# Order within the steps of a one-core attention and MLP kernel: magnitudes behind the activation, k'v copied out a step later, normalisation a step behind its statistics, row loads together, jobs at other steps

## The chip, the cores and the metric

One Trainium2 chip; the program runs on one core. The metric is the device time of that core in microseconds. Three runs of the kernel before gave 1775.66 to 1778.61 us, median 1776.37 us.

## The reference

All tensors are float32. Three stages follow each other (cut to what is computed):

```python
# q, k, v: (8 batches, 8 heads, 576 rows, 64); g_norm: (64,)
kv  = einsum('bhsd,bhse->bhde', k, v)
out = einsum('bhsd,bhde->bhse', q, kv)
x   = out / sqrt(mean(out*out, -1) + 1e-6) * g_norm      # heads side by side: (8, 576, 512)

u   = x + real(fft(fft(x, axis=1), axis=2))
un  = (u - mean(u)) / sqrt(var(u) + 1e-6)                # over the 512 columns
x   = u + relu(un @ moe_w_ch1) @ moe_w_ch2               # 512 -> 2048 -> 512

u   = x + (x^T @ U @ V)^T                                # over the 576 rows, rank 32
out = u + relu(u @ moe2_w_ch1) @ moe2_w_ch2              # 512 -> 2048 -> 512
```

The weights of the first MLP are drawn eight times larger than those of the second.

## The kernel before

The 8 x 576 = 4608 rows are cut into nine blocks of 512 (`NB = 9`). The first MLP takes one block in 16 steps (`NF = 16`), one step for 128 of the 2048 hidden columns. The steps are counted through: block j, step i is n = 16 j + i.

In step n TensorE first multiplies the normalised block by 128 columns of the first weight (`emit_l1(n)`, 12 matmuls of 128x512 into `h`), and then adds the product of the step before to the output (`emit_l2(n - 1)`, into four `acc` banks that live for the whole block). A product of two float32 matrices is made of three products of split operands (L224 to L226 and L253 to L255): a high part that ScalarE rounds off (`w1h`, `w2h`, `gh`, `xh`) and a remainder (`w1l` on POOL, in some steps on DVE; `w2l`, `gl`, `xl` on DVE). For the steps in the list `PLAIN`, the second product is not split: ScalarE makes one `g` (L229), TensorE multiplies four float32 pairs (L245), and no `w2h`, `w2l`, `gl` is made.

Every other stage is cut into small tasks that stand in the list `side[n]` and are emitted at the end of step n, behind `emit_l2(n - 1)`; `fill[n]` stands ahead of `emit_l2(n - 1)`. While block j is in the MLP, the tasks of batch j + 1 run: q times k'v (`o`, L358), its norm (squares L360, sums L365, power on POOL L367, scaling L376 and L378), the Fourier transform by folds (`f`, `e`, `eh`, `ez`) and two table products (`t_s1`, L437 to L443; `t_s2`, L469 to L471) whose parts are added up (`y`, `de`, `x`) and stored to HBM as `u_d`. At the end of a block the next block's rows are loaded back (`t_ln_load`: `un<-u_d`), their mean and variance taken (`t_ln_stats`, L577 and L578), normalised (`t_ln`: power on POOL L583, `un` L585) and transposed (`t_tr`: `tr` L595, then `xh` and `xl`). `t_kv` multiplies k' by v for a later batch (10 matmuls for each half, L298) and copies the diagonal blocks out to `kvbd` (ScalarE L302, DVE L306). The side products share two PSUM banks.

The first weights come as 64-bit words and are converted in the kernel: `w_mags` takes the magnitude of the low word on ScalarE (L113, L114), `convert` puts the parts together on DVE (L122 to L130) and POOL (L130), and `w_next` starts the load of a later piece. `w_conv` does this for the first MLP in the side tasks of block 0; `w_pre` does it for the second MLP's weights in steps `PRE` of the blocks 1 to 6 and stores the result (`wb_d`). From block 7 on the rank-32 stage and the second MLP run beside the rest; a `job` combines outputs that are needed for it in three side tasks of successive steps (DVE L878, L883, L893).

The order on each engine is the order in which the program emits: no scheduler reorders it, and each engine takes its instructions in turn. So a task that stands earlier in a list holds up everything behind it on its engines. TensorE, ScalarE (ACT), VectorE (DVE), GpSimd (POOL) and the DMA queue on SyncE (SP) run beside each other and wait by semaphores.

The last blocks of the program are one more block of 16 steps for the second MLP and four `group` passes for the rest of its rows.

Of the kernel before, what the change touches and what calls it, by code (L numbers as in the profile page):

```python
# [34 lines left out]
EARLY = (2, 3, 4)  # L35
PLAIN = (0, 1, 2, 3, 4, 5, 6, 7, 8, 12, 13)

# [8 lines left out]
def kernel(ctx: ExitStack, tc: tile.TileContext, qT, kvm, gn, w1a, w2a, w1b, w2b,  # L46
# [111 lines left out]
    def w_conv(*ss):  # L158

        convert(*((raws.pop(s), w_new(s), pws.pop(s)) for s in ss))  # L160
        w_next(ss)
        w_mags(*(s + 2 for s in ss if s + 2 < 2 * NF))

    pws = {}

    def w_mags(*ss):
        for s in ss:
            pws[s] = conv_0(raws[s], s % 4 > 1)
# [121 lines left out]
    kvbd = com.tile([128, 4, 128], F32, tag="kvbd", name="kvbd")  # L290

    def t_kv(b, half):
        kv = st[b]["kv"]
        ps = side_bank(f"kv{b}_{half}")
        for j in range(2):
            cols = slice(256 * half + 128 * j, 256 * half + 128 * j + 128)
            for t in range(KC):
                nc.tensor.matmul(out=ps[:, 128 * j:128 * j + 128], lhsT=kv[:, 0, t, cols], rhs=kv[:, 1, t, cols],  # L298
                                 start=(t == 0), stop=(t == KC - 1))
        pv = ps[:, 0:256].rearrange("p (j e) -> p j e", j=2)  # L300
        pairs = slice(2 * half, 2 * half + 2)
# [201 lines left out]
    def batch_tasks(b):  # L503
# [14 lines left out]
        for p in range(2):  # L518
            t[8 if d else 7 + p] += [lambda p=p, e=e: t_s1(b, p, e) for e in range(2)]
        if b + 1 < B:  # L520
            if b + 1 in EARLY:
                t[11].insert(0, lambda: kv_back(b + 1))
            else:
                t[7].append(lambda: load_kv(b + 1))
                t[11].insert(0, lambda: t_kv(b + 1, 0))
                t[12].insert(0, lambda: t_kv(b + 1, 1))
            t[12].append(lambda: load_q(b + 1))
# [25 lines left out]
    def t_ln_load(j):  # L553
        un_new(j)
        for t in range(4):
            load_u(un[j][t], 4 * j + t)
# [554 lines left out]
    side = {n: [] for n in range(-NF, NA + NF)}  # L1111
    CONV = 13
    on_dve = set()
    ONDVE = (3, 4)
    PRE = (0, 9, 12)
    SH = 1
# [5 lines left out]
    with tc.manual_schedule():  # L1122
# [16 lines left out]
        def conv(k):  # L1139
            nonlocal done  # L1140
            for _ in range(k):
                w_conv(done, done + 1)
                done += 2

        t_kv(0, 0)
# [50 lines left out]
        side[3].append(lambda: kv_load_early(4, 11))  # L1196
        fill = {n: lambda b=b, h=h: t_kv_early(b, h) for n, b, h in ((7, 4, 0), (8, 4, 1))}

        for j in range(NB):
            n0 = j * NF  # L1200
            if j + 1 < NB:
                side[n0 + 12].append(lambda j=j: t_ln_load(j + 1))
                side[n0 + 13].append(lambda j=j: (t_ln_stats(j + 1, range(4)), t_ln(j + 1)))
            if j + 1 < B:
                place(batch_tasks(j + 1), n0)
                on_dve |= {n0 + k for k in ONDVE if j}
            side[n0 + 13].append(lambda j=j: [t_res(j, t) for t in range(4)])
        side[7 * NF].append(lambda: t_mu(0))
# [4 lines left out]
        for e in range(4):  # L1213
            side[NA + 11 + e].append(lambda e=e: t_xsum(NB, e))
        place(prep_b(0), NA - NF)
        starts = [7 * NF + k for k in (5, 7, 9, 14)] + [8 * NF + k for k in (1, 3, 5, 7, 9, 11, 13, 15)] + \
                 [NA + k for k in (1, 3, 5, 7)]
        for k, n in enumerate(starts):
# [22 lines left out]
        for c in range(4):  # L1241
            side[NA + 12 + c].append(lambda c=c: v_load(c))
        for k, m in enumerate(range(done, 2 * NF, 2)):
            side[k * CONV * 2 // (2 * NF - done)].append(lambda m=m: w_conv(m, m + 1))
        spots = [NF * j + i for j in range(1, 8) for i in PRE]
# [11 lines left out]
        for n in range(NP):  # L1257
            i, j = n % NF, n // NF
            split_w2(n)
            emit_l1(n)  # L1260
            if n + 2 < NP:
                split_w1(n + 2)
# [134 lines left out]
```

## Time and profile before

| | |
|---|---|
| median of three runs | 1776.37 us |
| the profiled execution | 1777.05 us, of it the traced span 1775.1 us |
| TensorE busy in the span | 1717.9 us (97%) |
| DVE, ACT, POOL busy | 1187.7, 824.4, 464.6 us |
| mean granted TensorE clock | 0.987 of full speed |
| chain of waits, share of the span | TensorE 78%, DVE 12%, DMA 3%, ACT 3% |

TensorE is busy nearly all the time, so a microsecond is to be had where it stands idle, where its clock is granted at the lower level, or where it is given less work. Its idle time adds up to 57 us, 39 us of that in the first 205 us. Times in the rows are in microseconds from the start of the span. A row of a stretch of instructions gives the start, the duration, the engine, the line, the operation with the tiles it writes and reads, how many like instructions in a row it stands for, and in brackets how long the engine was idle before and what ended that.

### The profile page before, as it was taken

To read this page: it belongs to the slowest core of one execution; us is meant where nothing else is said; L and a number is where in the kernel's file an instruction comes from. 1 tells how busy PE (TensorE), PEld (TensorE's weight loads), DVE (VectorE), ACT (ScalarE), POOL (GpSimd) and SP (SyncE) were. 2 spreads that over 40 slices of the span, in tenths; PEclk is the share of its full clock that TensorE was granted. 3 is DMA by queue.
4 is the path that set the end of the run, shared out by engine and by line. 5 is a ranking of instruction groups with operands and counts; after the bars stand their busy time and mean duration, and the time that the engine had idled before them with its cause. 6 is when DMAs were issued, how large, how long until landed. Compare 5 with 4: busy or idle time off the path is not lost.

```text
span 1775.1 us, 22909 instructions
## 1 busy us (share of the span) xinstructions
PE 1717.9 (97%) x8092; PEld 1421.3 (80%) x8092; DVE 1187.7 (67%) x1906; ACT 824.4 (46%) x1579; POOL 464.6 (26%) x368
## 2 busy tenths in 40 slices
PE   5888999999999999999999999999999999999999
PEld 5657688888888888888888878888888888888887
DVE  5777777868667585774476676637934873595286
ACT  3565444544444344443445465355535644453343
POOL 2454445554444554444222222100000000000000
PEclk7999999999999999999999999999999999999999
DMA  9654305133242413402258885567785776677676
GB/s 372 242 178 148 139 24 186 51 117 119 107 151 96 165 69 119 150 1 87 78 184 301 289 306 196 184 204 224 232 280 176 250 254 207 212 239 240 197 224 192
DMA packets 129683, 318.97 MB, mean 180 GB/s; under 512 B 20680, under 2 KB 23512, under 8 KB 127328
## 3 DMA queue, kind: packets, MB, share of 16 engines
q1 hardware_dynamic: 129568, 317.51, 53.5%
q8 instruction: 64, 1.05, 0.2%
q14 instruction: 51, 0.42, 0.1%
HBM read 241.52 MB, written 77.57 MB: 180 GB/s over the span
## 4 chain that ended last, share of the span: by engine, by line
PE 78%; DVE 12%; DMA 3%; ACT 3%; issue 2%; POOL 2%; SPq 0%; ACTq 0%; DVEq 0%; POOLq 0%
PE y L1020 10%; PE yy L1100 10%; PE h L224 6%; PE h L225 6%; PE h L226 5%; PE acc L253 5%; PE acc L255 5%; PE acc L254 5%; PE z L1100 5%; PE zz L1020 5%; PE w L1100 2%; PE z L1020 2%; DVE f L397 2%; PE o L358 2%; DVE f L392 1%
## 5 line engine op out<-in xcount | busy, mean ns | idle before, releaser
L200 POOL TENSOR_TENSOR w1l<-w,w1h 128x512 fp32r<-128x512 f32 x148 | 200.1, 1352 | 434.3 <-ACT w1h L199 417.5
L224 PE MATMUL h<-xl,w1h 128*128 128x512 f32 x576 | 230.6, 400 | 1.4 <-DVE xl L600 1.4
L226 PE MATMUL h<-xh,w1l 128*128 128x512 f32 x576 | 225.0, 391 | 0.5 <-POOL w1l L200 0.5
L225 PE MATMUL h<-xh,w1h 128*128 128x512 f32 x576 | 225.3, 391 | 0.0
L253 PE MATMUL acc<-w2h,gl 128*128 128x512 f32 x532 | 210.1, 395 | 8.7 <-DVE gl L234 8.6
L255 PE MATMUL acc<-w2h,gh 128*128 128x512 f32 x532 | 207.7, 390 | 0.0
L254 PE MATMUL acc<-w2l,gh 128*128 128x512 f32 x532 | 207.7, 390 | 0.0
L1020 PE MATMUL y<-xv,v 128*128 128x512 f32 x768 | 187.4, 390 | 2.7 <-ACT g L957 2.7
L233 ACT ACTIVATE gh<-h 128x512 fp32r<-128x512 f32 x149 | 88.5, 594 | 193.3 <-PE h L226 180.2
L957 ACT ACTIVATE g<-y 128x512 f32<-128x512 f32 x128 | 76.6, 598 | 204.0 <-PE y L1020 204.0
L1020 PEld LDWEIGHTS y<-xv,v 128*128 128x128 f32 x768 | 143.8, 188 | 34.1 <-ACT g L957 4.4
L234 DVE SCALAR_TENSOR_TENSOR gl<-h,gh 128x512 fp32r<-128x512 f32 x149 | 102.1, 685 | 87.8 <-ACT gh L233 86.6
L210 DVE TENSOR_TENSOR w2l<-w,w2h 128x512 fp32r<-128x512 f32 x149 | 132.0, 886 | 23.5 <-ACT w2h L209 22.6
L226 PEld LDWEIGHTS h<-xh,w1l 128*128 128x128 f32 x576 | 108.5, 188 | 24.3 <-POOL w1l L200 0.9
L224 PEld LDWEIGHTS h<-xl,w1h 128*128 128x128 f32 x576 | 108.7, 189 | 23.7 <-DVE xl L600 1.8
L253 PEld LDWEIGHTS acc<-w2h,gl 128*128 128x128 f32 x532 | 100.3, 188 | 33.4 <-DVE gl L234 13.2
L225 PEld LDWEIGHTS h<-xh,w1h 128*128 128x128 f32 x576 | 108.8, 189 | 21.7 <-issue 1.4
L255 PEld LDWEIGHTS acc<-w2h,gh 128*128 128x128 f32 x532 | 100.2, 188 | 21.1
L254 PEld LDWEIGHTS acc<-w2l,gh 128*128 128x128 f32 x532 | 100.3, 189 | 20.1
L199 ACT ACTIVATE w1h<-w 128x512 fp32r<-128x512 f32 x160 | 99.7, 623 | 24.0 <-DVE w L130 24.0
L209 ACT ACTIVATE w2h<-w 128x512 fp32r<-128x512 f32 x149 | 92.9, 623 | 37.0 <-PE acc L255 33.5
L951 DVE TENSOR_TENSOR g<-zz,g 128x512 f32<-128x512 f32 x64 | 44.2, 691 | 89.8 <-ACT g L957 77.4
(219 smaller groups left out, 3642.1 us busy)
## 6 DMA issues: line engine op xcount, KB each, us to landing
v<-wv_d SPq DMA_DIRECT2D x224, 512.0 KB, 4.1
wv_d<-vo SPq DMA_DIRECT2D x112, 256.0 KB, 2.7
kv<-in_kvm SPq DMA_DIRECT2D x8, 1280.0 KB, 8.1
q<-in_qT SPq DMA_DIRECT2D x8, 1220.0 KB, 9.6
x_d<-x2o SPq DMA_DIRECT2D x36, 256.0 KB, 2.0
x2f<-x_d SPq DMA_DIRECT2D x36, 256.0 KB, 5.5
outT<-o SPq DMA_DIRECT2D x36, 256.0 KB, 2.7
u_d<-x SPq DMA_DIRECT2D x32, 256.0 KB, 2.8
```

Source lines behind the costliest of these rows:

```text
L199: nc.scalar.activation(out=ah, in_=a, func=AF.Copy)
L200: (nc.vector if n in on_dve else nc.gpsimd).tensor_tensor(out=al, in0=a, in1=f32(ah), op=ALU.subtract)
L210: nc.vector.tensor_tensor(out=cl, in0=c, in1=f32(ch), op=ALU.subtract)
L224: nc.tensor.matmul(out=h, lhsT=ah[:, kc, :], rhs=xl[:, kc, :], start=(kc == 0), stop=False)
L225: nc.tensor.matmul(out=h, lhsT=ah[:, kc, :], rhs=xh[:, kc, :], start=False, stop=False)
L226: nc.tensor.matmul(out=h, lhsT=al[:, kc, :], rhs=xh[:, kc, :], start=False, stop=(kc == 3))
L234: nc.vector.scalar_tensor_tensor(out=gl, in0=h, scalar=0.0, in1=f32(gh), op0=ALU.max, op1=ALU.subtract)
L253: nc.tensor.matmul(out=a, lhsT=gl[:, tt], rhs=ch, start=s, stop=False)
L254: nc.tensor.matmul(out=a, lhsT=gh[:, tt], rhs=cl, start=False, stop=False)
L255: nc.tensor.matmul(out=a, lhsT=gh[:, tt], rhs=ch, start=False, stop=e)
L1020: nc.tensor.matmul(out=dst, lhsT=w[:, c], rhs=r[:, k], start=p in (0, 1, 3) and k + n == 0, stop=k == 1 and n == 2, skip_group_check=True)
L1100: nc.tensor.matmul(out=dst[mp], lhsT=w[:, c], rhs=r, start=p in (0, 1, 6, 3) and i + n == 0, stop=i == 7 and n == 2, skip_group_check=True)
```

## The change

Eight edits, all to the order or to where a task stands; one of them (`PLAIN`) also changes the form of a product.

1. `PLAIN` gets steps 14 and 15: in block 0 their second product is four float32 matmuls.
2. `w_conv` no longer calls `w_mags` for the pieces two on. For the conversions of block 0's steps 1 to 9, `w_mags` stands in its own step, right behind `emit_l1(n)`, so behind the step's `g`. The conversions of block 0 are one a step.
3. `t_kv` is cut in two: the matmuls stand at the end of `side[11]` and `side[12]`, the copies at the start of `side[12]` and `side[13]` (for batches 5, 6 and 7, in blocks 3, 4 and 5).
4. Batch 4's early k'v (`t_kv_early`) stands in `fill[6]` and `fill[7]`, before in 7 and 8.
5. In block 0 the second pass of `t_s1` stands in `fill[9]`, ahead of `emit_l2(8)`, before at the end of step 8.
6. `PRE` is (7, 9, 12), before (0, 9, 12).
7. `t_ln_load` stands at the end of step 11 (before step 12); `t_ln_stats` stays in step 13; `t_ln` stands in step 14 (before behind the statistics in 13).
8. The jobs start in block 7 at steps 5, 7, 9, 11, 13 (before 5, 7, 9, 14), in block 8 as before, and in the block after at 1, 4, 8 (before 1, 3, 5, 7).

```diff
-PLAIN = (0, 1, 2, 3, 4, 5, 6, 7, 8, 12, 13)
+PLAIN = (0, 1, 2, 3, 4, 5, 6, 7, 8, 12, 13, 14, 15)
...
         w_next(ss)
-        w_mags(*(s + 2 for s in ss if s + 2 < 2 * NF))
...
+    kvps = {}
+
     def t_kv(b, half):
+        t_kv_mm(b, half)
+        t_kv_out(b, half)
+
+    def t_kv_mm(b, half):
         kv = st[b]["kv"]
-        ps = side_bank(f"kv{b}_{half}")
+        ps = kvps[b, half] = side_bank(f"kv{b}_{half}")
...
-        pv = ps[:, 0:256].rearrange("p (j e) -> p j e", j=2)
+
+    def t_kv_out(b, half):
+        pv = kvps.pop((b, half))[:, 0:256].rearrange("p (j e) -> p j e", j=2)
...
         for p in range(2):
-            t[8 if d else 7 + p] += [lambda p=p, e=e: t_s1(b, p, e) for e in range(2)]
+            if d and p:
+                fill[9] = lambda: [t_s1(b, 1, e) for e in range(2)]
+            else:
+                t[7 + d + p] += [lambda p=p, e=e: t_s1(b, p, e) for e in range(2)]
...
-                t[11].insert(0, lambda: t_kv(b + 1, 0))
-                t[12].insert(0, lambda: t_kv(b + 1, 1))
+                for h in range(2):
+                    t[11 + h].append(lambda h=h: t_kv_mm(b + 1, h))
+                    t[12 + h].insert(0, lambda h=h: t_kv_out(b + 1, h))
...
-    PRE = (0, 9, 12)
+    PRE = (7, 9, 12)
...
-        fill = {n: lambda b=b, h=h: t_kv_early(b, h) for n, b, h in ((7, 4, 0), (8, 4, 1))}
+        for n, h in ((6, 0), (7, 1)):
+            fill[n] = lambda h=h: t_kv_early(4, h)
...
-                side[n0 + 12].append(lambda j=j: t_ln_load(j + 1))
-                side[n0 + 13].append(lambda j=j: (t_ln_stats(j + 1, range(4)), t_ln(j + 1)))
+                side[n0 + 13].append(lambda j=j: t_ln_stats(j + 1, range(4)))
+                side[n0 + 14].append(lambda j=j: t_ln(j + 1))
...
+            if j + 1 < NB:
+                side[n0 + 11].append(lambda j=j: t_ln_load(j + 1))
...
-        starts = [7 * NF + k for k in (5, 7, 9, 14)] + [8 * NF + k for k in (1, 3, 5, 7, 9, 11, 13, 15)] + \
-                 [NA + k for k in (1, 3, 5, 7)]
+        starts = [7 * NF + k for k in (5, 7, 9, 11, 13)] + [8 * NF + k for k in (1, 3, 5, 7, 9, 11, 13, 15)] + \
+                 [NA + k for k in (1, 4, 8)]
...
-            side[k * CONV * 2 // (2 * NF - done)].append(lambda m=m: w_conv(m, m + 1))
+            side[k].append(lambda m=m: w_conv(m, m + 1))
+            if k:
+                mags[k] = m, m + 1
...
             emit_l1(n)
+            if n in mags:
+                w_mags(*mags[n])
```

ScalarE, block 0, steps 1 and 2, before (`cv` and `raw` or `more_raw` are the magnitudes of two pieces, `g` the step's activation, `w1h` the high part for two steps on, `sq` the squares of batch 1):

```order
L113 ACTIVATE cv_727<-raw 128x512
L114 ACTIVATE raw<-raw 128x512
L113 ACTIVATE cv_730<-raw 128x512
L114 ACTIVATE raw<-raw 128x512
L229 ACTIVATE g_746<-h_733 128x512
L199 ACTIVATE w1h_748<-w_0_3_715 128x512
L360 ACTIVATE sq_761<-o_0_763 128x512
L360 ACTIVATE sq_761<-o_1_773 128x512
```

The same steps in the changed kernel:

```order
L228 ACTIVATE g_740<-h_727 128x512
L113 ACTIVATE cv_742<-raw 128x512
L114 ACTIVATE raw<-raw 128x512
L113 ACTIVATE cv_745<-raw 128x512
L114 ACTIVATE raw<-raw 128x512
L198 ACTIVATE w1h_748<-w_0_3_715 128x512
L367 ACTIVATE sq_761<-o_0_763 128x512
L367 ACTIVATE sq_761<-o_1_773 128x512
```

The activation has moved ahead of the four magnitude instructions; the high part `w1h` and the squares stand behind both, as before.

TensorE, block 3, the end of step 11, before (`kv_0` is the first half of k'v of batch 5, `s_4_2` the last part of the second table product of batch 4, in the two side banks):

```order
L255 MATMUL acc_3_3733<-w2h_4206,gh_4223 128x512
L298 MATMUL kv_0_4304<-kv_4063 128x128 x10
L469 MATMUL s_4_2_0_4317<-tab_196,y_4040 34x258
L470 MATMUL s_4_2_0_4317<-tab_196,y_4040 34x258
L471 MATMUL s_4_2_0_4317<-tab_196,y_4040 34x258
```

and in the changed kernel:

```order
L476 MATMUL s_4_2_1_4283<-tab_196,y_3990 34x258
L477 MATMUL s_4_2_1_4283<-tab_196,y_3990 34x258
L478 MATMUL s_4_2_1_4283<-tab_196,y_3990 34x258
L303 MATMUL kv_0_4300<-kv_4013 128x128 x10
L223 MATMUL h_4320<-xl_3542,w1h_4199 128x512
```

The ten k'v matmuls have moved from ahead of the table product to behind it, so the bank that they take is the one that the product has just filled; the next step's `h` stands right behind them.

DVE, the end of block 7, before (`ln` and `un` are the normalisation of block 8, `job` and `vo` the jobs, `w2l` and `gl` the remainders of steps 14 and 15, `xl` the remainder of the transposed block):

```order
L582 TENSOR_SCALAR ln_1_8117<-ln_2_8116 128x4
L585 TENSOR_SCALAR un_8067<-un_8067,ln_2_8116,ln_1_8117 128x512 x4
L210 TENSOR_TENSOR w2l_8145<-w_0_14_1510,w2h_8144 128x512
L234 SCALAR_TENSOR_TENSOR gl_8162<-h_8148,gh_8161 128x512
L210 TENSOR_TENSOR w2l_8182<-w_0_15_1569,w2h_8181 128x512
L234 SCALAR_TENSOR_TENSOR gl_8199<-h_8185,gh_8198 128x512
L600 TENSOR_TENSOR xl_8207<-tr_0_8208,xh_8206 128x4x128
```

and in the changed kernel, from the second stage of the fourth job on:

```order
L894 TENSOR_TENSOR vo_0_0_8056<-job_0_7955,vo_0_0_8056 128x256 x2
L894 TENSOR_TENSOR vo_0_1_8057<-job_1_7956,vo_0_1_8057 128x256
L209 TENSOR_TENSOR w2l_8133<-w_0_14_1516,w2h_8132 128x512
L233 SCALAR_TENSOR_TENSOR gl_8150<-h_8136,gh_8149 128x512
L593 TENSOR_SCALAR ln_1_8107<-ln_2_8106 128x4
L596 TENSOR_SCALAR un_7998<-un_7998,ln_2_8106,ln_1_8107 128x512 x4
L904 TENSOR_TENSOR vo_1_0_8128<-job_2_7957,vo_1_0_8128 128x2x256
L904 TENSOR_TENSOR vo_1_1_8129<-job_3_7958,vo_1_1_8129 128x2x256
L889 TENSOR_TENSOR job_8065<-job_8065 128x256 x4
L209 TENSOR_TENSOR w2l_8191<-w_0_15_1569,w2h_8190 128x512
L233 SCALAR_TENSOR_TENSOR gl_8208<-h_8194,gh_8207 128x512
L611 TENSOR_TENSOR xl_8216<-tr_0_8217,xh_8215 128x4x128
```

The normalisation has moved behind `w2l` and `gl` of step 14, and the last stage of one job (two instructions) and the first stage of the next (four) stand between it and `w2l`, `gl` and `xl` of step 15.

## Rows read from the trace of the kernel before

**Rows 1.** Waits of TensorE by line, 66 to 205 us: us in total, times, longest.
```profile
PE acc L245 <- ACT g L229: 5.1, 4, 1.9
PE s L437 <- ACT kvbd L338: 3.7, 1, 3.7
PE tr L595 <- DVE un L585: 2.6, 2, 2.3
PE acc L253 <- DVE gl L234: 1.0, 1, 1.0
```

**Rows 2.** Waits of TensorE by line, 200 to 1060 us, the first.
```profile
PE acc L253 <- DVE gl L234: 7.6, 10, 1.0
```

**Rows 3.** Two stretches: busy us of PE, PEld, DVE, ACT, POOL, PEclk, DMA, GB/s.
```profile
140.00:150.00 10.00, 5.70 (x22) 5.18 (x23) 5.92 (x13) 5.51 (x13) 2.69 (x2) 0.67 0.42 119
190.00:200.00 10.00, 6.40 (x24) 4.53 (x23) 8.73 (x16) 2.31 (x4) 3.66 (x3) 0.73 0.46 183
```

**Rows 4.** TensorE in order of time, at seven places.
```profile
108.89 5.40 PE L245 MATMUL acc<-w,g 128*128 128x512 f32 x8 [1.94 <-ACT g L229]
118.39 3.70 PE L245 MATMUL acc<-w,g 128*128 128x512 f32 x8 [1.37 <-ACT g L229]
...
144.83 0.61 PE L437 MATMUL s<-tab,eh 128*128 128x290 f32 x1 [3.69 <-ACT kvbd L338]
...
194.91 1.12 PE L595 MATMUL tr<-ident,un 128*128 128x128 f32 x4 [2.31 <-DVE un L585]
...
244.31 0.50 PE L253 MATMUL acc<-w2h,gl 128*128 128x512 f32 x1 [0.72 <-DVE gl L234]
...
491.15 0.40 PE L224 MATMUL h<-xl,w1h 128*128 128x512 f32 x1
...
492.78 0.40 PE L225 MATMUL h<-xh,w1h 128*128 128x512 f32 x1
...
514.30 0.50 PE L253 MATMUL acc<-w2h,gl 128*128 128x512 f32 x1 [0.78 <-DVE gl L234]
```

**Rows 5.** ScalarE in order of time, at three places.
```profile
115.37 0.68 ACT L113 ACTIVATE cv<-raw 128x512 f32<-128x512 f32 x1 [1.51 <-DMA raw<-in_w1a]
...
144.22 0.55 ACT L338 ACTIVATE kvbd<-kve 64x128 f32<-64x128 f32 x2
...
269.54 0.66 ACT L113 ACTIVATE cv<-raw 128x512 f32<-128x512 f32 x1
...
491.49 0.38 ACT L473 ACTIVATE de<-s 34x258 f32<-34x258 f32 x1 [1.45 <-PE s L471]
```

**Rows 6.** DVE in order of time, at seven places.
```profile
139.04 0.42 DVE L426 TENSOR_TENSOR eh<-f,eh 128x256 fp32r<-128x256 f32 x1 [2.85 <-ACT eh L413]
...
188.74 0.70 DVE L577 BATCH_NORM_STATS2 ln<-un 128x6 f32<-128x512 f32 x1 [2.30 <-DMA un<-u_d]
...
217.21 1.76 DVE L210 TENSOR_TENSOR w2l<-w,w2h 128x512 fp32r<-128x512 f32 x1
...
235.82 0.69 DVE L210 TENSOR_TENSOR w2l<-w,w2h 128x512 fp32r<-128x512 f32 x1 [1.35 <-ACT w2h L209]
...
892.61 1.30 DVE L893 TENSOR_TENSOR vo<-job,vo 128x512 fp32r<-128x512 f32 x2
...
926.92 1.29 DVE L600 TENSOR_TENSOR xl<-tr,xh 128x512 fp32r<-128x512 f32 x2 [0.32 <-ACT xh L599]
...
928.58 1.09 DVE L878 TENSOR_TENSOR job<-job,job 128x256 f32<-128x256 f32 x3
```

**Rows 7.** SP's queue: the rows' load in block 0, pieces behind `w_pre` in block 1.
```profile
182.20 1.74 SPq L543 DMA_DIRECT2D un<-u_d  x3
...
278.22 0.33 SPq L102 DMA_DIRECT2D raw<-in_w1b  x1
```

**Rows 8.** DMA issues: KB each, median us from issue to landing.
```profile
raw<-in_w1b SPq DMA_DIRECT2D x16, 512.0 KB, 4.2
u_d<-x SPq DMA_DIRECT2D x8, 64.0 KB, 1.6
```

More of the change, by code (lines that the diff above doesn't have):

```diff
@@ L1111 @@
     side = {n: [] for n in range(-NF, NA + NF)}
-    CONV = 13
+    fill = {}
     on_dve = set()
     ONDVE = (3, 4)
-    PRE = (0, 9, 12)
+    PRE = (7, 9, 12)
     SH = 1
@@ L1143, in conv @@
                 done += 2
+                w_mags(done, done + 1)
         t_kv(0, 0)
@@ L1242 @@
             side[NA + 12 + c].append(lambda c=c: v_load(c))
+        mags = {}
         for k, m in enumerate(range(done, 2 * NF, 2)):
-            side[k * CONV * 2 // (2 * NF - done)].append(lambda m=m: w_conv(m, m + 1))
+            side[k].append(lambda m=m: w_conv(m, m + 1))
+            if k:
+                mags[k] = m, m + 1
         spots = [NF * j + i for j in range(1, 8) for i in PRE]
```

## The prediction

> **What bounds the kernel now.** I read the table of busy times first: TensorE works in 97% of the span, so nothing that only relieves another engine counts unless TensorE waits for it. Then the waits of TensorE by line, for block 0 with what precedes it and for the rest apart. Up to 205 us there are four kinds worth a term: the plain second product waits for `g` (5.1 us, four times), the table product waits for the copy `kvbd` (3.7 us, once), the transposes wait for `un` (2.6) and the second product of step 14 for `gl` (1.0) [rows 1]. From 200 to 1060 us nearly all is one kind, the second product waiting for `gl`, ten times, 7.6 us together [rows 2]. In order of time six of the ten are step 5 of blocks 1 to 6, 0.72 to 0.75 us each, the first at 244.31, and three are the ends of blocks 3, 4 and 5, 0.76 to 0.78 us each, the first at 514.30 [rows 4]. The tenth lies in block 7, behind work that the change leaves where it is. The waits past 1060 us, too.
>
> The third view is the granted clock. It falls behind the long waits: 0.67 in the stretch from 140 to 150 us, which holds the wait of 3.69 us, and 0.73 from 190 to 200 us, which holds those of 2.31 for `un` and 1.0 for `gl` [rows 1, 3, 4]. What a wait costs can be read off where the same eight plain matmuls run twice: 5.40 us at 108.89, 3.70 us at 118.39 [rows 4]. So a wait that goes gives back more than its own length. The fourth view is each engine in order of time at these places; the rest of the text takes it up.
>
> **Block 0, steps 1 to 9.** Before the change ScalarE comes to `g` behind four magnitude instructions, and these wait for a DMA: 1.51 us at 115.37, with the other magnitudes and `g` behind [rows 5]. Now `g` stands ahead of them, so the four waits for `g`, 5.1 us, and the 1.7 us of lower clock behind one of them can go. They are not the sum, though. Nothing is taken off DVE: it converts the same pieces, normalises the same batch, and comes to the Fourier inputs when it comes to them; at 139.04 it waits itself, 2.85 us, for the `eh` of ScalarE, and the table product follows it [rows 6]. The magnitudes stand ahead of `w1h` in both orders, so the ring magnitudes, conversion, `w1h`, norm, folds is as long as before. TensorE then comes earlier to the table product and waits there for what it no longer waits for at `g`. I credit nothing for the waits ahead of 140 us.
>
> Behind 140 us the wait for `kvbd` goes: its copy stood at 144.22 behind a conversion [rows 5], and with batch 4's early k'v one step earlier and the second pass of the table product in `fill[9]`, the copy is long done. That is 3.69 us [rows 4], and the lower clock behind it: of the 10 us in the stretch, at 0.67, 6.6 us are at 1.2 GHz; if the whole wait lies in them 2.9 us of work ran at half speed and lost 1.5 us, if none does 3.3 us, so 2.4 in the middle [rows 3]. Together at most 6.1 us. But conversion, the folds' last part and the copies are still to be done by the same two engines, and what is late next is the second pass's `ez` on DVE. Bounds: 0 (a new wait takes all) to 6.1, or about 12 with the waits for `g`. I take 3.5, nearest to the row of the wait itself.
>
> **Block 0, the end.** The load of the rows for block 1 is issued at 182.20 behind two raw loads of 512 KB [rows 7]; DVE waits 2.30 us for it at 188.74 [rows 6]. Now it is issued ahead of them. It still waits for the last store of `u_d`, which takes 1.6 us to land [rows 8]: the issue itself moves by under a microsecond, but the 1 MB that was ahead in the queues is behind. So the wait of 2.30 goes and with it most of the 2.31 that the transposes wait. Steps 14 and 15 lose their four instructions on DVE (two `w2l`, two `gl`) and two copies on ScalarE, so the 1.0 for `gl` goes, and of the 2.6 for `un` the rest (0.29). That is 3.6 us of waits [rows 1, 4], and the lower clock: 0.73 over 10 us withholds 2.7 us [rows 3], of which between 0.9 and 2.7 fell on work, and it goes on a little past 200 us; I take 2.6. Against that the plain form is longer: eight passes take 3.70 us to the modelled end of the last, some 3.5 to the start of what follows, against 12 matmuls that start 0.233 us apart (eight from 491.15 to 492.78, seven distances), 2.8 us [rows 4]; so 0.7 us for each of two steps, 1.4 us. Net 3.6 + 2.6 - 1.4 = 4.8 us; bounds -1.4 (waits stay) and 6.5.
>
> Here a rule of the Trainium skill speaks against the change. The row gives 1.6 us from issue to landing for these stores [rows 8]. The skill's Perfetto Trace Analysis, section DMA Instruction — HWDGE (DVE, Sync), says that the semaphore is raised only once the last write is confirmed, and that this can take surprisingly long where the target is HBM, as here. By the rule the load that now stands right behind the store could start late, and hold back the raw loads behind it; then the term would be 4.8 less the 2.3 of the wait, 2.5 us. The time of the row already ends with that semaphore, so I keep 4.8.
>
> **Step 5 of blocks 1 to 6.** DVE runs through the block's first five steps to the wait at 244.31 with one stop, 1.35 us at 235.82 [rows 4, 6], and that one goes back to DVE too (ScalarE's copy there waits for DVE's norm). In that chain stand the six DVE instructions of `w_pre` in step 0, and the `w2l` behind them, beside POOL's two of `w_pre`, takes 1.76 us at 217.21 instead of the 0.69 at 235.82 [rows 6]. The 1.07 us of that alone are more than the wait of 0.73, the six instructions come on top: all six waits go, 6 x 0.73 = 4.4 us. Bounds 0 and 4.4. In step 7 DVE stands idle several times for ScalarE's parts of the table product, and what `w2l` and `gl` make there is used a whole step later; that hides the move, and I cost it at 0 (at most the same 0.73 per block if that cover were gone).
>
> **k'v in blocks 3, 4 and 5.** At the block's end the wait for `gl` is `un`, `w2l`, `gl` in a row on DVE (the four of `un` ahead), late because a k'v copy made DVE and ScalarE late on the step before. With the copies one step on and the normalisation behind the step's `w2l` and `gl`, the wait goes: 3 x 0.77 = 2.3 us; bounds 1 and 2.3. But the matmuls now stand behind the second table product and take its bank, which ScalarE copies out only from 491.49 to 491.87 [rows 5], while TensorE went on to the next step at 491.15 [rows 4]: 0.7 us of new wait in each of three blocks, 2.0 us (bounds 0.3, if another bank is free, and 2.5). What is behind these matmuls on TensorE is the next step's first product, so the wait is paid in full.
>
> **The end of block 7.** Between `un` and the last `w2l` come six instructions that stood elsewhere: two of L893 (1.30 us together) and four of L878 (0.41 and 1.09) [rows 6], 2.8 us. DVE was not idle there: `xl` at 926.92 waited only 0.32 us [rows 6]. `xl` then is done some 2.8 us later than at 928.2, and the second pair of transposes needs its banks, the next block's first product the `xl` behind them. I take 2.0 of these 2.8 us as loss, for TensorE had a little less than a microsecond to spare there; bounds 0 (if earlier instructions make room) and 4 (if the normalisation is late as well).
>
> **Sum.** 3.5 + 4.8 + 4.4 + 2.3 - 2.0 - 2.0 = 11.0 us. The profiled execution took 1777.05 us, which gives 1766.05; it lies 0.68 us above the median of the runs, so on the scale of the runs the forecast is 1765.4 us, 0.6% faster.
>
> **Rivals.**
> (a) The ring in block 0 keeps everything up to step 9: new waits for `ez` and `e` eat the 3.5. Then 1765.4 + 3.5 = 1769. For it: the ring is as long as before. Against: the wait at 144.83 is for a copy that moves away.
> (b) Block 0 gives all: the waits for `g` go and aren't paid again. The front then gives 12 instead of 3.5, so 1765.4 - 8.5 = 1757. For it: ScalarE's DMA waits are the visible cause. Against: DVE is the longer chain.
> (c) Block 0 doesn't do what it should at all: nothing at the front, and the rows come no earlier, so that the plain form is a pure loss of 1.4. Then 1765.4 + 3.5 + 4.8 + 1.4 = 1775, no change.
> (d) Slower: the raw pieces come late. From the magnitudes of `w_pre` in step 9 to the issue of the next pieces 8.7 us pass, 269.54 to 278.22 [rows 5, 7]. In step 7 the magnitudes would start some 14 us, two steps and a table product, ahead of those of step 9, so the issue is near 264 and the landing, 4.2 us on [rows 8], 1.3 us ahead of need; before, the pieces of step 0 had nine steps. ScalarE takes them in order, with `w2h` and `gh` of step 10 behind, which have some 2 us to spare. If they landed over 7.5 us after issue, TensorE would stand in each of five blocks for every microsecond beyond. The kernel is slower than before by 3.5 us from (11 + 3.5) / 5 = 2.9 us beyond, 10.4 us after issue; at 11.5 us it is 1765.4 + 5 x 4 = 1785. For it: one queue serves them, and k'v is loaded in the same step. Against: landing is 4.2 us, and the wait for magnitudes is ScalarE's, which has time to spare in most steps.
>
> **Chances.** Forecast (1759 to 1768) 0.68; (a) 0.15; (b) 0.07; (c) 0.05; (d) 0.05. About 0.2% (3.5 us) is what a measurement of this kernel can tell from no change. Faster by more: forecast, (a) and (b), 0.90, less 0.03 for cases in which several terms fail together: 0.87. Within: 0.08. Slower: 0.05. The range that leaves two in ten out goes from the far side of (b) to a little past (a): 1757.5 to 1772.
>
> **What would show it.** The waits for `gl` at step 5 of blocks 1 to 6 are gone; if they stand, that term is wrong. There is a wait of about 0.7 us of k'v for ScalarE at the end of step 11 in blocks 3 to 5, and none for `gl` at the blocks' ends. At the end of block 7 the transposes wait for `xl` or `un`. In block 0 the waits for `g` are under 1 us together, the wait for `kvbd` is gone, and waits for `e` or `ez` are longer than 0.9. Block 1 begins 7 to 10 us earlier. Wrong would be above all a first step of block 1 that comes at the same time, or waits of ScalarE for `raw` in blocks 1 to 5.

## The result, and the profile after

The changed kernel took 1761.18 us (median of 4 runs, 1757.8 to 1761.6) against 1776.91 us of the kernel before: ratio 0.9907, 95% interval 0.989 to 0.9924. That is 15.7 us or 0.9% faster; 1765.4 was forecast, with 1757.5 to 1772. The profiled execution took 1761.38 us (span 1759.4), 15.67 us less than the one before, so the two traces can be set beside each other step by step.

The handiest ruler is ScalarE's activation of the first product, one in each of the 16 steps of each block. Its start in the two traces (block/step, us from the start of the span):

| block/step | before | after | after less before |
|---|---|---|---|
| 0/0 | 73.64 | 71.99 | -1.65 |
| 0/15 | 192.69 | 186.48 | -6.21 |
| 1/0 | 209.20 | 197.86 | -11.34 |
| 2/0 | 312.12 | 299.67 | -12.45 |
| 3/0 | 415.04 | 401.54 | -13.50 |
| 4/0 | 523.73 | 508.78 | -14.95 |
| 5/0 | 632.43 | 616.00 | -16.43 |
| 6/0 | 741.13 | 723.24 | -17.89 |
| 7/0 | 844.04 | 825.10 | -18.94 |
| 7/15 | 925.28 | 906.39 | -18.89 |
| 8/0 | 935.23 | 920.37 | -14.86 |
| 9/15 | 1123.69 | 1108.04 | -15.65 |

What the last column gains or loses from one row to the next belongs to the stretch between them. In us this gives: start-up 1.65, steps of block 0 4.56, its end 5.13; then 1.05 at step 5 of each of blocks 1 to 6 (6.3 together), 1.09 at the end of each of blocks 3 to 5 (3.3), less 0.68 in each of these three at the new place of k'v (2.05); 4.03 lost at the end of block 7; 0.8 won after it.

One profile of each kernel stands behind these differences, and they scatter from profile to profile. The steps of block 0 gain 4.9 to 5.4 us in the eight other profiles below that have the same order there (e2, e5 to e10, e12); the end of block 0 was 0.8 us shorter in e1, whose block 0 is that of the kernel before.

The waits of TensorE from 66 to 205 us (us in total, times, longest), which answer to [rows 1]:

```profile
PE h L225 <- POOL w1l L199: 2.8, 2, 2.3
PE o L365 <- DVE x L369: 1.9, 1, 1.9
PE s L444 <- DVE y L463: 1.5, 1, 1.5
PE s L448 <- DVE e L437: 1.2, 1, 1.2
PE h L223 <- ACT w1h L198: 1.0, 1, 1.0
PE acc L244 <- ACT g L228: 0.7, 1, 0.7
```

The waits for `g` are down from 5.1 to 0.7 us, and those for `kvbd`, `un` and `gl` are gone. In their place stand waits for `w1l`, `x`, `y` and `w1h`: the ring of conversion, split and norm, for which TensorE now comes too early.

The same from 206 to 920 us, which answers to [rows 2]:

```profile
PE tr L606 <- DVE xl L611: 2.1, 1, 2.1
PE kv L303 <- ACT de L480: 1.8, 3, 0.6
PE acc L252 <- DVE gl L233: 1.0, 1, 1.0
```

Of the ten waits for `gl` one is left, in block 7. The three of k'v and the one of the transposes are new.

Three stretches (busy us of PE, PEld, DVE, ACT, POOL, the granted clock, DMA share, GB/s), the first two as in [rows 3], the third the end of block 7:

```profile
140.00:150.00 10.00, 8.46 (x37) 5.62 (x36) 9.18 (x17) 7.55 (x16) 3.92 (x3) 1.00 0.48 158
190.00:200.00 10.00, 10.00 (x49) 7.10 (x48) 4.59 (x8) 3.62 (x7) 0.94 (x1) 1.00 0.14 52
908.00:918.00 10.00, 7.91 (x32) 6.21 (x31) 8.73 (x16) 3.45 (x6) 1.18 (x1) 0.83 0.57 220
```

Block 0's two stretches of low clock, 0.67 and 0.73 before, are at full clock; the end of block 7 has a new one.

TensorE in order of time, at the places of [rows 4]: step 5 of block 1, k'v in block 3, and the end of block 7.

```profile
231.81 0.39 PE L225 MATMUL h<-xh,w1l 128*128 128x512 f32 x1
232.04 0.39 PE L252 MATMUL acc<-w2h,gl 128*128 128x512 f32 x1
...
474.97 2.50 PE L303 MATMUL kv<-kv 128*128 128x128 f32 x20 [0.61 <-ACT de L480]
...
911.99 1.72 PE L606 MATMUL tr<-ident,un 128*128 128x128 f32 x8 [2.09 <-DVE xl L611]
913.35 0.78 PE L252 MATMUL acc<-w2h,gl 128*128 128x512 f32 x1
913.93 0.63 PE L253 MATMUL acc<-w2l,gh 128*128 128x512 f32 x1
```

At step 5 the second product now starts 0.23 us behind the last matmul of the first, with no wait. Behind the wait of 2.09 us the matmuls take 0.63 us each instead of 0.39: the lower clock.

DVE at the end of block 7, from the last stage of one job to `xl`:

```profile
906.40 1.29 DVE L904 TENSOR_TENSOR vo<-job,vo 128x512 fp32r<-128x512 f32 x2
907.60 2.53 DVE L889 TENSOR_TENSOR job<-job 128x256 f32<-128x256 f32 x4
910.05 0.68 DVE L209 TENSOR_TENSOR w2l<-w,w2h 128x512 fp32r<-128x512 f32 x1
910.66 0.68 DVE L233 SCALAR_TENSOR_TENSOR gl<-h,gh 128x512 fp32r<-128x512 f32 x1
911.26 0.67 DVE L611 TENSOR_TENSOR xl<-tr,xh 128x512 fp32r<-128x512 f32 x1
```

The six job instructions take 3.65 us here, from 906.40 to 910.05, and the first `xl` ends just before the transposes at 911.99.

### The profile page after: what moved, and what is told of

Its sections match the earlier page's. It is cut to its first block, busy times and chain, and to the rows that moved or that the text cites. A ratio compares the mean times of both kernels' runs of the same rounds, so it can differ in the third digit from the quotient of the medians.

```text
span 1759.4 us, 22914 instructions
## 1 busy us (share of the span) xinstructions
PE 1709.4 (97%) x8084; PEld 1414.5 (80%) x8084; DVE 1177.1 (67%) x1902; ACT 824.1 (47%) x1577; POOL 461.2 (26%) x368
## 3 DMA queue, kind: packets, MB, share of 16 engines
q8 instruction: 64, 1.05, 0.2%
## 4 chain that ended last, share of the span: by engine, by line
PE 85%; DVE 2%; DMA 1%; POOL 1%; ACT 1%; issue 1%; SPq 0%; DVEq 0%; ACTq 0%; POOLq 0%
PE y L1031 10%; PE yy L1111 10%; PE h L223 7%; PE h L224 7%; PE h L225 7%; PE acc L252 6%; PE acc L253 6%; PE acc L254 6%; PE z L1111 5%; PE zz L1031 5%; PE w L1111 2%; PE z L1031 2%; PE o L365 2%; PE pt L727 1%; PE u L752 1%; PE kv L303 1%
## 5 line engine op out<-in xcount | busy, mean ns | idle before, releaser
L252 PE MATMUL acc<-w2h,gl 128*128 128x512 f32 x524 | 205.8, 393 | 1.0 <-DVE gl L233 1.0
L209 DVE TENSOR_TENSOR w2l<-w,w2h 128x512 fp32r<-128x512 f32 x147 | 127.1, 865 | 26.4 <-ACT w2h L208 25.7
```

Of the source, the lines that this page charges most:

```text
L209: nc.vector.tensor_tensor(out=cl, in0=c, in1=f32(ch), op=ALU.subtract)
L252: nc.tensor.matmul(out=a, lhsT=gl[:, tt], rhs=ch, start=s, stop=False)
```

## The experiments

Each ran beside the kernel before on the same chip. Single runs of one kernel lie some 5 us apart, so verdicts on a microsecond are taken from the ruler above, one profile each, as the change from one row to a later one, and the times are given beside them. What the ruler gains or loses is against the changed kernel, if nothing else is said. The ratios alone do not bear out the small gains: none of those of e2, e5, e8 and e12 (0.9907 to 0.9921) lies below the changed kernel's 0.9907, and the intervals reach some 0.0015 to either side.

**e1: `w_pre` moved, alone.**

```diff
# on the kernel before
-    PRE = (0, 9, 12)
+    PRE = (7, 9, 12)
```

> The kernel before with one edit alone: w_pre in steps 7, 9, 12 instead of 0, 9, 12. Theory (the waits of step 5 are DVE's, and w_pre in step 0 makes them): the six waits for gl at step 5 of blocks 1 to 6 go, each worth 1.05 us from one step's activation to the next (0.73 us of idle, 0.16 us by which a matmul's row overlaps the next one's start, and some 0.15 us of slower start), so 6.3 us, time near 1770.5. Rival 1 (a wait is worth only its idle): 4.4 us, 1772.5. Rival 2 (the wait comes from the rest of DVE's chain in steps 0 to 5, or the pieces of step 9 now come late): under 2 us, 1775 or more, and a wait of ScalarE for raw in blocks 1 to 5.

1769.12 us against 1775.76, ratio 0.9969 (0.9959 to 0.998). On the ruler, against the kernel before, step 5 gives 1.05 us in each of blocks 1 to 6, 6.3 together. Of the ten waits of [rows 2] four are left:

```profile
PE acc L253 <- DVE gl L234: 3.3, 4, 1.0
```

The theory holds, and with it the price of a wait: more than its idle. The first activation, at 0/0, comes 1.38 us earlier here too, though nothing before it differs from the kernel before. Two more places move that the edit doesn't touch: the end of block 0 is 0.8 us shorter (the clock from 190 to 200 us was 0.83, against 0.73), and block 9 loses 1.95 us (0.70 from 1035 to 1045 us).

**e2: the jobs' old starts in the changed kernel.**

```diff
-        starts = [7 * NF + k for k in (5, 7, 9, 11, 13)] + ...
-                 [NA + k for k in (1, 4, 8)]
+        starts = [7 * NF + k for k in (5, 7, 9, 14)] + ...
+                 [NA + k for k in (1, 3, 5, 7)]
```

> The changed kernel with the job starts of the kernel before (block 7: 5, 7, 9, 14; the block after: 1, 3, 5, 7). Theory (the six job instructions between un and the last xl make the second transposes late, and the wait of 2.1 us takes the clock down for 3.4 us more): 4.0 us less, 1757.1, no wait of the transposes for xl at the end of block 7 and no low clock there. Rival (the normalisation in step 14 is late by itself): a wait of about 1 us stays at the transposes, gain under 2 us, 1759.5 or more.

1758.11 us, ratio to before 0.9907 (0.9892 to 0.9921). At the end of block 7 the ruler gains 4.04 us, all that the changed kernel had lost there; 0.5 of it is given back past 1020 us. The transposes wait for nothing:

```profile
906.26 1.03 PE L606 MATMUL tr<-ident,un 128*128 128x128 f32 x8
...
909.88 1.03 PE L606 MATMUL tr<-ident,un 128*128 128x128 f32 x8
```

So there is no loss without the jobs: the normalisation in step 14 costs nothing by itself. It has a part in the loss beside them (e8).

**e3: the magnitudes ahead of `g` again.**

```diff
         w_next(ss)
+        w_mags(*(s + 2 for s in ss if s + 2 < 2 * NF))
...
-            if k:
-                mags[k] = m, m + 1
```

> The changed kernel with the magnitudes of block 0 where they stood before (end of the step before, ahead of g); all else as changed. Theory of the prediction (the order of the magnitudes gives nothing by the end of step 9, since DVE's chain to the table product is as long): the waits for g come back, 4 to 5 us up to step 6, but step 10 of block 0 begins at most 1 us later and the time is near 1762. Rival (the waits for g are the gain): step 10 begins 4 to 5 us later, the time is near 1766.

1762.04 us, ratio to before 0.9933 (0.9916 to 0.9949). At the end of block 0 the ruler has lost 2.73 us, of which 1.81 was there at 0/0: 0.9 us for the magnitudes. On the way there it had lost up to 7.5 (at step 1, where the activation itself stands behind the magnitudes; 5.7 at step 6). Against the eight other profiles with the changed front it is 1.3 to 1.8 us. The waits of TensorE, 66 to 205 us:

```profile
PE acc L245 <- ACT g L229: 4.2, 3, 2.0
PE s L449 <- DVE e L438: 2.8, 1, 2.8
PE h L226 <- POOL w1l L200: 1.9, 2, 1.3
```

The waits for `g` are back with 4.2 us, and others have shrunk for them. The prediction's theory holds in the main: of the 5 us of waits for `g` 0.9 to 1.8 are a gain by the end.

**e4: early k'v and the second pass of the table product at their old places.**

```diff
-            if d and p:
-                fill[9] = lambda: [t_s1(b, 1, e) for e in range(2)]
-            else:
-                t[7 + d + p] += [...]
+            t[8 if d else 7 + p] += [...]
...
-        for n, h in ((6, 0), (7, 1)):
+        for n, h in ((7, 0), (8, 1)):
```

> The changed kernel with batch 4's early k'v in steps 7 and 8 again and block 0's second pass of the first table product at the end of step 8. Theory of the prediction (the front's gain is the copy of kvbd that no longer holds the table product): the wait for kvbd comes back with 3 to 4 us and low clock behind it, the time is near 1765. Rival (the magnitudes behind g are the gain; the copy is earlier because of them): under 1.5 us lost, 1762 or less.

1767.17 us, ratio to before 0.9957 (0.9943 to 0.9972). The ruler loses 4.9 us between steps 2 and 10 of block 0 and no more after; counted from 0/0 it is 4.0, for the changed kernel's profile comes to 0/0 earlier and gives 0.8 us of that back (in step 2 TensorE waits 1.85 us for `x` there and 1.0 here). The old wait is there to the hundredth, with the lower clock behind it (0.44 us rows where the full clock has 0.30):

```profile
139.79 0.40 PE L448 MATMUL s<-tab,e 97*128 97x290 f32 x1 [1.26 <-DVE e L437]
140.03 0.29 PE L450 MATMUL s<-tab,ez 97*128 97x290 f32 x1
144.02 0.61 PE L444 MATMUL s<-tab,eh 128*128 128x290 f32 x1 [3.69 <-ACT kvbd L345]
144.43 0.44 PE L445 MATMUL s<-tab,eh 128*128 128x290 f32 x1
```

**e5: the k'v matmuls one product later.**

```diff
-                    t[11 + h].append(lambda h=h: t_kv_mm(b + 1, h))
+                    fill[NF * (b - 1) + 12 + h] = lambda h=h: t_kv_mm(b + 1, h)
                     t[12 + h].insert(0, lambda h=h: t_kv_out(b + 1, h))
```

> The changed kernel with the k'v matmuls of blocks 3, 4 and 5 in fill of steps 12 and 13 (behind the next first product, ahead of emit_l2) instead of at the end of steps 11 and 12; the copies stay at the start of the side tasks of steps 12 and 13. Theory (the matmuls wait 0.61 us for the bank that the table product filled, 0.68 us from step to step): three waits go, 2.0 us less, 1759.1. Rival (the wait only moves: the copies, now one product behind their matmuls, make DVE late at the block's end): the waits for gl at the ends of blocks 3 to 5 come back, 1 us each, and the time is 1761 to 1762.

1759.86 us, ratio to before 0.9916 (0.9899 to 0.9932). The ruler gains 0.87 us in each of blocks 3, 4 and 5, 2.6 together; no wait of k'v is left, and none for `gl` comes back.

**e6: steps 14 and 15 of block 0 split again.**

```diff
-PLAIN = (0, 1, 2, 3, 4, 5, 6, 7, 8, 12, 13, 14, 15)
+PLAIN = (0, 1, 2, 3, 4, 5, 6, 7, 8, 12, 13)
```

> The changed kernel with steps 14 and 15 of block 0 split again, as before. Theory of the prediction (the plain form costs 1.4 us of TensorE and is paid by the waits for un and gl that it removes, 1.3 us of idle and the low clock behind it): waits of 1 to 2 us come back at the end of block 0, the time is 1761 to 1764. Rival (with the rows loaded early DVE has room for the four instructions, and the plain form is a pure loss): no wait there, 1.4 us less, 1759.8.

1762.99 us, ratio to before 0.9934 (0.9919 to 0.9948). On the ruler the end of block 0 is the same to 0.1 us (1.39 us behind at 0/15, 1.48 in block 1). Waits of 0.9 us in sum come back, and about as much is saved on the shorter product:

```profile
188.37 1.11 PE L606 MATMUL tr<-ident,un 128*128 128x128 f32 x8 [0.60 <-DVE un L596]
...
192.51 0.66 PE L606 MATMUL tr<-ident,un 128*128 128x128 f32 x4 [0.27 <-DVE xl L611]
```

Neither theory has its size; by itself the plain form is worth nothing here.

**e7: the rows loaded in step 12, behind everything of that step.**

```diff
-                side[n0 + 11].append(lambda j=j: t_ln_load(j + 1))
+                side[n0 + 12].append(lambda j=j: t_ln_load(j + 1))
```

> The changed kernel with the rows loaded at the end of step 12 again. Theory (in block 0 the rows come late behind two raw loads): DVE waits 2 us for un at the end of block 0, the transposes start about 2 us late and the clock falls behind it, 2 to 4 us more, 1763 to 1765; nothing changes at the ends of the other blocks. Rival (the skill's rule on the confirmation of writes to HBM, or the load is hidden anyway): no wait for un in either place, 1761.

1769.71 us, ratio to before 0.9973 (0.9962 to 0.9983): 7.5 us lost at the end of block 0, far more than expected. In this place the load stands behind two raw loads and also behind the load of `q`, 1220 KB. SP's queue, then DVE:

```profile
174.72 0.36 SPq L102 DMA_DIRECT2D raw<-in_w1b  x1
175.49 0.35 SPq L102 DMA_DIRECT2D raw<-in_w2b  x1
175.94 0.38 SPq L500 DMA_DIRECT2D q<-in_qT  x1
176.37 4.20 SPq L554 DMA_DIRECT2D un<-u_d  x5
```

```profile
186.91 0.69 DVE L588 BATCH_NORM_STATS2 ln<-un 128x6 f32<-128x512 f32 x1 [5.93 <-DMA un<-u_d]
```

The issue is 2.5 us later than in the changed kernel, and DVE comes to the rows 6.8 us later (0.7 of both is this run's later arrival at the step). So not the step but what stands ahead in the queue costs most; e10 tells the two apart.

**e8: the normalisation in step 13 again.**

```diff
-                side[n0 + 13].append(lambda j=j: t_ln_stats(j + 1, range(4)))
-                side[n0 + 14].append(lambda j=j: t_ln(j + 1))
+                side[n0 + 13].append(lambda j=j: (t_ln_stats(j + 1, range(4)), t_ln(j + 1)))
```

> The changed kernel with the normalisation behind the statistics in step 13 again. Theory (the ends of blocks 3 to 5 gain 1.09 us each because un no longer stands ahead of w2l and gl of step 14): the three waits for gl come back, 3.3 us more, 1764.5; at the end of block 7 un is earlier and some of the 4 us lost there come back. Rival (these waits went because the k'v copies moved): no wait at the ends of blocks 3 to 5, the time is 1761 or less.

1761.19 us, ratio to before 0.9921 (0.9906 to 0.9936). At the ends of blocks 3 to 5 nothing changes; at the end of block 7 the wait for `xl` is 1.1 us instead of 2.1 and the ruler gains 2.6 us:

```profile
PE tr L606 <- DVE xl L611: 1.1, 1, 1.1
```

Of the 2.6 us 1.0 is the shorter wait and the rest the clock, which was at 1.00 from 909 to 919 us here and 0.83 in the changed kernel's profile. The rival is right: those three waits stay away with the normalisation in step 13, and in block 7 its step 14 costs beside the jobs, about 1.0 us of wait.

**e9: k'v as in e5 and the jobs as in e2.**

> The changed kernel with the k'v matmuls of blocks 3 to 5 in fill of steps 12 and 13 and with the job starts of the kernel before. Theory (the two places are independent): 2.6 and 4.0 us less, and 0.5 us given back past 1020 us, so about 1755. Rival (they share DVE's chain or the gain is given back behind block 7): 1758, no better than the jobs alone.

1755.17 us, ratio to before 0.9889 (0.9874 to 0.9903). On the ruler it gains 6.7 us from the start of block 1 to the start of block 8 (from 0.62 us behind the changed kernel to 6.10 ahead) and 6.3 by 9/15, so the two places add up: 2.6 and 4.0. By the ratios, 0.9889 against 0.9907, it is 3 us, and the intervals overlap; some 1.5 us of the ruler's gain is the clock at the end of block 7, which does not fall in every run (last section). Its waits of TensorE from 206 to 1020 us:

```profile
PE acc L252 <- DVE gl L233: 1.0, 1, 1.0
PE acc L256 <- DVE w2l L209: 0.5, 1, 0.5
```

**e10: the rows loaded at their exact old place.**

```diff
+                side[n0 + 12].append(lambda j=j: t_ln_load(j + 1))      # ahead of the step's side tasks
...
-                side[n0 + 11].append(lambda j=j: t_ln_load(j + 1))      # behind the step's side tasks
```

> The changed kernel with the rows' load in step 12 and ahead of that step's side tasks, its exact place in the kernel before (so behind the two raw loads, but ahead of the 1220 KB of q that the run with 7.5 us of loss had in front, too). Theory (what is ahead in the queue decides, by its bytes: 1 MB now, 2.2 MB there): DVE waits some 2 us for un, the block's end is 2 to 4 us later than in the changed kernel, 1763 to 1765. Rival (the step is what matters, not the queue): 7 us, 1768 or more.

1761.48 us, ratio to before 0.9923 (0.9908 to 0.9937). The ruler loses 0.87 us at the end of block 0 (from 1.96 to 2.83 us behind), less than theory and rival had. DVE waits 1.63 us for the rows, and 0.65 of it comes through to TensorE:

```profile
189.00 1.11 PE L606 MATMUL tr<-ident,un 128*128 128x128 f32 x8 [0.65 <-DVE un L596]
```

The two raw loads are ahead in both, and the step is the same; so `q` ahead in the queue made most of the 7.5 us of e7.

**e11: edits 4 and 5 alone.**

```diff
# on the kernel before: t_kv_early in fill 6 and 7, the second pass of t_s1 in fill[9]
```

> The kernel before with two edits alone: batch 4's early k'v one step earlier and block 0's second pass of the first table product in fill of step 9. Theory (these two give the front's gain, the magnitudes next to nothing): step 10 of block 0 comes 3.5 to 5 us earlier than in the kernel before at the same start, time 1771 to 1773. Rival (it takes the magnitudes behind g as well): under 2 us, 1774 or more.

1772.51 us against 1775.73, ratio 0.9985 (0.9975 to 0.9995). On the ruler, against the kernel before, 3.3 us are won from 0/0 to 0/15 (from 1.37 behind to 1.91 ahead), and the block's end is the old one, to 0.01 us on the ruler and in its waits:

```profile
PE tr L598 <- DVE un L588: 2.2, 2, 1.5
PE acc L253 <- DVE gl L234: 1.0, 1, 1.0
```

The two edits make most of the front's 4.56 us by themselves; 3.3 here and 0.9 to 1.8 in e3 make it up within the scatter. No run tells edit 4 from edit 5.

**e12: k'v whole and in steps 11 and 12, the normalisation in step 14.**

```diff
-                for h in range(2):
-                    t[11 + h].append(lambda h=h: t_kv_mm(b + 1, h))
-                    t[12 + h].insert(0, lambda h=h: t_kv_out(b + 1, h))
+                t[11].insert(0, lambda: t_kv(b + 1, 0))
+                t[12].insert(0, lambda: t_kv(b + 1, 1))
```

> The changed kernel with the k'v of blocks 3 to 5 whole and at the start of steps 11 and 12, as before; the normalisation stays in step 14. Theory (the waits for gl at these blocks' ends went because the copies moved, as the run with the normalisation in step 13 has it): the three waits come back with 1.09 us each, the three waits of the k'v matmuls, 0.68 us each, go: 1.2 us more, 1762.4. Rival (either edit alone removes the waits for gl): only the waits of the matmuls go, 2.0 us less, 1759.1.

1759.74 us, ratio to before 0.9916 (0.9902 to 0.9931). Each of blocks 3 to 5 gains 0.69 us at step 12 and loses 0.36 of it at its end, where the kernel before had lost 1.09; no wait for `gl` of half a microsecond is left. So with e8: either edit alone removes most of those waits or all, and splitting k'v, on top of the normalisation in step 14, loses 0.33 us a block.

## Why the prediction was right

The time lay in the range, 4.2 us below the forecast. Of the signs that the prediction named all came but one: block 1 began 11.3 us earlier (9.7 without the start), not 7 to 10. Point by point, forecast and trace in microseconds:

| term | forecast | trace |
|---|---|---|
| block 0, steps 1 to 9 | 3.5 | 4.56 (to step 15) |
| block 0, the end | 4.8 | 5.13 |
| step 5 of blocks 1 to 6 | 4.4 | 6.3 |
| ends of blocks 3 to 5 | 2.3 | 3.3 |
| k'v behind the table product | -2.0 | -2.05 |
| end of block 7 | -2.0 | -4.03 |
| past block 7 | 0 | 0.8 |
| start-up | 0 | 1.65 |
| sum | 11.0 | 15.66 |

The nearness of the sum is in part luck: what the waits for `gl` gave beyond their terms (1.9 and 1.0) and what block 7 lost beyond its own (2.0) have opposite signs, and the last two rows are chance or clock (see below).

**Front of block 0.** The step held: "I credit nothing for the waits ahead of 140 us" is nearly what e3 shows (0.9 to 1.8 us of 5.1), and that the gain hangs on the wait for the copy `kvbd` is what e4 and e11 show (4.0 to 4.9 us lost, 3.3 won). The new wait that was to eat part of it is there: 1.54 us for `y`, not for `ez`, and ahead of it 2.3 for `w1l` in step 6.

**End of block 0.** The size was right, the working only in part, so the near hit (5.13 for 4.8) is partly luck. The prediction took the early load and the plain form as two parts of one sum. Undone singly each is worth next to nothing (0.9 us in e10, 0.1 in e6), while neither is there in e11, whose end of block 0 is that of the kernel before. That reads as two remedies for one wait: DVE's chain to `un` and `gl` had to get some 3 us shorter, and either nearly does it. It is an inference: no run undoes just these two together, and in e11 the magnitudes and the normalisation are at their old places as well (e8 has the latter worth 0.1 us there). The plain form's longer product, put at 1.4 us, was thus paid for almost nothing. The upper bound of 6.5 does not come out of the rows either: 3.6 us of waits, 2.7 of clock and 0.7 more of it past 200 us (0.64 from 200 to 202), less 1.4, are 5.6.

The Trainium skill's rule on the confirmation of HBM writes (Perfetto Trace Analysis, DMA Instruction — HWDGE (DVE, Sync)) would have put this term at 2.5 us. No run here shows it:

```profile
173.54 0.32 SPq L496 DMA_DIRECT2D u_d<-x  x1
173.92 2.69 SPq L554 DMA_DIRECT2D un<-u_d  x5
```

```profile
180.13 0.69 DVE L588 BATCH_NORM_STATS2 ln<-un 128x6 f32<-128x512 f32 x1
```

The five are the rows' loads. The first is issued 0.38 us behind the last store, they take 2.69 us to issue, and DVE, which had waited 2.30 us, comes to the rows without a wait. Before, the first stood 2.43 us behind that store, and the five took 2.69 us too ([rows 7] has the first three of them):

```profile
179.77 0.33 SPq L489 DMA_DIRECT2D u_d<-x  x1
182.20 2.69 SPq L543 DMA_DIRECT2D un<-u_d  x5
```

So the issue moved by 2 us against the last store, not by less than one. And none of the loads had to wait for that store: in the kernel's code the last store (L496) writes rows 544 to 575 of batch 1, and the loads of block 1 read its rows 0 to 447. The last store that they do read from was issued at 171.61, 2.3 us ahead of the first of them. So the prediction's wait for the last store wasn't there, before or after, and the rule isn't put to the test.

**Step 5.** The mechanism was right (e1), the term was mis-sized: six times the idle of 0.73 us instead of 1.05. TensorE in the kernel before, around the wait of [rows 4]:

```profile
243.21 0.39 PE L226 MATMUL h<-xh,w1l 128*128 128x512 f32 x1
244.31 0.50 PE L253 MATMUL acc<-w2h,gl 128*128 128x512 f32 x1 [0.72 <-DVE gl L234]
244.66 0.40 PE L254 MATMUL acc<-w2l,gh 128*128 128x512 f32 x1
```

The row of a matmul lasts 0.39 us, while without a wait the next starts 0.23 us after it (231.81 and 232.04 in the changed kernel); the idle is counted from the end of the row, so 0.16 us of every such wait is not in it. And the first matmul behind a wait is followed after 0.35 us, not 0.23. Together 0.73 + 0.16 + 0.12 = 1.01 of the 1.05. The same holds for the 0.77 us at the ends of blocks 3 to 5, which were worth 1.09; there the reason given was too narrow as well, since either of the two edits does it or nearly (e8, e12). The k'v term held in place and size, and e5 gives it back.

**End of block 7.** The forecast named the instructions and the transposes that wait for `xl`, and the wait of 2.09 us is the 2.0 it took. It left out what such a wait had cost everywhere else in its own working: the clock. The four job instructions (2.53 us) also ran 1 us longer than the rows that they were priced by (0.41 and 1.09). The bound of 4 us was the value in this profile. In e3, e7, e10 and e12, with the same order there and the same wait of 2.09 us, the clock did not fall, and the same stretch lost 2.5 us.

**Rivals.** (a) and (b) failed: the ring kept less than all and gave less than all. (c) is refuted by the table. Of (d) nothing is seen: ScalarE waits for no raw piece in blocks 1 to 6, and in block 1 it takes those of step 9 straight behind `de`:

```profile
256.81 0.39 ACT L480 ACTIVATE de<-s 128x258 f32<-128x258 f32 x1 [3.05 <-PE s L478]
257.09 0.66 ACT L113 ACTIVATE cv<-raw 128x512 f32<-128x512 f32 x1
```

**What isn't the change.** The 1.65 us at 0/0 lie ahead of any instruction that moved. Of the first 60 us 0.81 was the clock in the profile before and 0.86 in the profile after; but it was 0.86 in e1, whose start is that of the kernel before, and 0.82 in e4, whose start is that of the changed kernel and which comes to 0/0 1.95 us later. So 1.65 us of the profiles' difference is chance; without it the edits give 14.0. Past block 7 the profile before has a stretch at 0.83 behind a wait that is nearly the same after (2.6 and 2.7 us for `x2s`) at full clock; I take most of the 0.8 us for that. e8, whose order there is the changed kernel's, has the same wait of 2.7 us with a low clock behind it, and loses 1.0 us there:

```profile
1030.00:1040.00 10.00, 8.29 (x29) 6.67 (x30) 6.91 (x11) 8.20 (x15) 2.12 (x2) 0.83 0.82 304
```

## What to carry to other kernels

Price a wait of TensorE by what lies behind it, not by its idle: a row's overlap with the next, the slow first matmul and, behind some of the longer waits, the clock; here 0.73 us of idle were worth 1.05, and 2.09 us were worth 2.5 or, with the clock, 4.0. When two edits shorten the same chain, do not add their worth: undo each alone in the changed kernel, and drop the one that costs something. A task that is moved to the end of a block has to be laid beside what runs there already; the same job instructions were free behind `xl` and cost 2.5 to 4 us in front of it.

## What the runs showed of the hardware

The same wait doesn't always cost the same. The transposes at the end of block 7 wait 2.1 us in eight of the profiles, in the same instruction order; in the profile of the changed kernel the clock fell behind it (0.83 over 10 us, shown above), in that of e12 it did not:

```profile
905.00:915.00 10.00, 7.91 (x42) 6.28 (x42) 9.97 (x19) 5.93 (x11) 1.60 (x1) 1.00 0.42 162
```

The low clock was there in the changed kernel, e4, e5 and e6, and not in e3, e7, e10 and e12, which lose 1.5 us less than the former at that place on the ruler. What decides it no run shows. This and the start are a part of the scatter of some 5 us between runs of one kernel, which is more than several of the edits are worth.
